# Second layer of an MLP in 64x64 quarters of the array, inside the attentions of the next batch

## The chip, the core and the metric

The kernel runs on one core of a Trainium2 chip. A core has TensorE (matmuls; in the profile PE, with its weight loads as PEld), VectorE (DVE), ScalarE (ACT), GpSimd (POOL) and SyncE (SP, which here only issues DMAs), each with an instruction queue of its own that is worked off in order; queues wait for one another through semaphores. Matmuls write to PSUM, which has eight banks of 512 float32 per partition, and an engine must read a result out of its bank before the bank takes another. The metric is the device time of one execution in microseconds (us).

## What is computed

Attention with normalised q and k over 8 batches and 12 heads (448 tokens, head size 64), and an MLP with tanh-GELU on its output:

```python
q_n, k_n = rmsnorm(q, g_q), rmsnorm(k, g_k)              # over the 64 of a head
attn = softmax(q_n @ k_n.T / sqrt(64))
x = (attn @ v)                                           # laid out as (3584 tokens, 768)
out = gelu_tanh(x @ w_in) @ w_out                        # 768 -> 2048 -> 768, float32 out
```

## The kernel before

Batches b = 0 to 7 run one after the other. A batch has an attention and a first layer; its second layer is worked off inside the attention of the next batch. `manual_schedule` is on: each engine's order is the order in which the code issues.

An attention (`attention`, L501; batch 0 has its own, `first_attention`) has 21 *units* (`unit`, L315): chunk c = 0 to 2 of four heads, key block t = 0 to 6. A unit is four matmuls of 64 rows x 64 columns of the array with 448 moving columns each, one per quarter of the array, into a two-bank tile `sc`; then one `exp` on ACT over both banks (896 elements per partition). When a chunk has its seven units, `products(b, c, 0)` sums the keys (matmuls with ones; where `key_sums` has added the keys on DVE before, only one group of four matmuls is left) and `products(b, c, 1)` multiplies with v: seven groups of four quarter matmuls. `turned`, `recips` and `quad_x` make x from them on DVE: two transposes, a reciprocal, a transpose, a multiplication into `xT`.

The first layer (`mm1_pair` L468, `mm1` L413) uses the full array, 128x128, six matmuls of 448 columns for each of 16 blocks f; a gelu on ACT writes g. The first two pairs of blocks use two-bank tiles, blocks 4 to 15 use one bank each from the pool `ps_m`.

The second layer (`mm2`, L434) has seven tiles of 128 tokens for two batches, three from an even batch and four from an odd one. For each tile and each half of the 768 output columns there are 16 full-array matmuls of 384 columns into one bank of `ps_m`, a copy to `osb` (L448 on DVE, L446 on ACT) and, after the second half, two DMAs on SP (L456). `m2_parts` makes a list of these matmuls, one *step* each; `attention` takes 96 (b = 1) or 112 (b = 2 to 7) of them from the list through `upto`, between the groups of units, in shares that are written out (`first`, `last`, `tail`, `shares`). Since an odd batch gives 128 steps and an even one 96, the attentions of batches 3, 5 and 7 begin in the middle of a list.

PSUM after the first batch: two single banks (`ps_m`) for the second layer and blocks 4 to 15 of the first, three two-bank tiles t0 to t2 (`rounds`) for units, products, the first two pairs of the first layer and a scratch tile in `rsqrt_last`. `pair` hands them out in turn:

```python
rounds.append(rounds.pop(0))
return rounds[-1]
```

The last batch's second layer (144 matmuls, L434) runs by itself at the end.

SP's queue holds, in the order of issue, the loads of q and k (L119), the transposes by DMA (L305) and the stores (L456).

Of the kernel before, what the change touches and what calls it, by code (L numbers as in the profile page):

```python
# [17 lines left out]
def kernel(  # L18
# [20 lines left out]
    R = 64  # L39
# [131 lines left out]
    roots, places = {}, {}  # L171
# [65 lines left out]
    def rsqrt_last(b):  # L237
# [3 lines left out]
        own = pair("root")[:, :, :4 * NT]  # L241
# [6 lines left out]
        for i in range(3):  # L248
            nc.vector.tensor_copy(z, y)
            nc.vector.tensor_mul(t, z, y)  # L250
            nc.vector.scalar_tensor_tensor(t, t, -0.5, ms, op0=ALU.mult, op1=ALU.mult)
            nc.vector.scalar_tensor_tensor(y, t, 1.5, y, op0=ALU.add, op1=ALU.mult)

# [61 lines left out]
    def unit(b, c, t):  # L315
# [12 lines left out]
        nc.scalar.activation(ex[:, t], sc[:, :, :S], AF.Exp, scale=scale, bias=shift)  # L328

# [29 lines left out]
    def products(b, c, what, lo=0, hi=NT):  # L359

        if lo == 0 and rounds:
# [19 lines left out]
    def turned():  # L381
        st = oas["st"] = stp.tile([128, 2, S // 32, 32], F32, tag="st", name="st")
        for r in range(2):
            nc.vector.transpose(st[:, r].rearrange("p a b -> p (a b)"), oas[0][r])  # L384

# [9 lines left out]
    def quad_x(b, c):  # L395
        if c == 0:
            xT[b] = xp.tile([128, HP, S], BF16, tag="xT", name="xT")
        if rounds:
            nc.vector.tensor_mul(
                xT[b][:, 2 * c:2 * c + 2], oas["o", 1][:, :, :S], oas["rb"]  # L400
            )
            return
# [5 lines left out]
    def mm1(b, f, cs=range(HP)):  # L408
        if cs[0] == 0:
            hs1["m"] = ps_m.tile([128, 512], F32, tag="mm", name="h")  # L410
        h = hs1["m"]
        for c in cs:
            nc.tensor.matmul(  # L413
                h[:, :S], win[:, c, f * 128:(f + 1) * 128], xT[b][:, c],
                start=(c == 0), stop=(c == HP - 1),
            )
        if cs[-1] < HP - 1:
            return
        nc.scalar.activation(  # L419
            g[:, f, (b % 2) * S:(b % 2 + 1) * S], h[:, :S], AF.Gelu_apprx_tanh  # L420
        )

    out_v = out.rearrange("(r t) d -> t r d", t=NT)
    osbs, by_act = {}, []

    def mm2(b, i, half, f, lo, hi):

        end = b + 1 == B and i + 1 == 2 * S // 128
# [4 lines left out]
        o, osb = osbs["ps"][:, :hi - lo], osbs[i]  # L433
# [6 lines left out]
        last = end and hi == d_model  # L440
        if last:

            nc.vector.tensor_copy(osb[:R, lo:hi], o[:R])
            nc.scalar.copy(osb[R:, lo:hi], o[R:])
        elif b + 1 == B and (lo == 0 or end) or by_act:
# [3 lines left out]
        if half == 0 and not end:  # L449
            return  # L450
        for j in range(2):
            col = i * 128 + j * R
            r = ((b // 2) * 2 + col // S) * R
            cols = slice(lo if end else 0, hi)
            eng = nc.scalar if last and j else nc.sync
            eng.dma_start(  # L456
                out_v[col % S // R, r:r + R, cols], osb[j * R:(j + 1) * R, cols]
            )

    def mm1_pair(i, cs=range(HP), b=0, js=range(2)):  # L460
# [11 lines left out]
        if cs[-1] == HP - 1 and js[-1] == 1:  # L472
            nc.scalar.activation(  # L473
                g[:, 2 * i:2 * i + 2, (b % 2) * S:(b % 2 + 1) * S], h[:, :, :S],
                AF.Gelu_apprx_tanh
            )

    early, late = range(HP - 2), range(HP - 2, HP)

    def m2_parts(b):  # L480
        tiles = range(3) if b % 2 == 0 else range(3, 7)
        order = [(i, half) for i in tiles for half in range(2)]
# [3 lines left out]
        parts = [(i, half, half * HD, (half + 1) * HD) for i, half in order]  # L486
        if b + 1 == B:
            i, half, lo, hi = parts.pop()
            parts += [(i, half, lo, lo + HD // 2), (i, half, lo + HD // 2, hi)]
        return [  # L490
            lambda part=part, f=f: mm2(b, part[0], part[1], f, *part[2:])
            for part in parts for f in range(nf)
        ]

    def attention(b, m2, quota, side, behind, ends):
# [3 lines left out]
        cuts = (0, 3, 6, 9, 11, 13, 16, 18, 21)  # L499
        groups = [units[i:j] for i, j in zip(cuts, cuts[1:])]  # L500
        first, last, tail = (23, 16, 4) if b > 1 else (18, 14, 3)  # L501
        sums_at, x_at = {3: 0, 6: 1}, {4: 0}
        shares = (0, 12, 24, 35, 45, 58, 69) if b > 1 else (0, 12, 25, 33, 41, 53, 61)
        spread = quota - first - last - tail
        given = 0

        def upto(k):
            nonlocal given
            while given < k:
                m2.pop(0)()  # L510
                given += 1

        before = []
        for i, group in enumerate(groups):
            for fn in side.get(i, ()):
                fn()
            if b == 1 and i == 3:
                by_act.append(b)
            for c, t in group:
                unit(b, c, t)  # L520
            for c, t in before:
                key_sums(b, c, t)
            if i in x_at:
                products(b, x_at[i], 1)
                quad_x(b, x_at[i])
            elif i in sums_at:
# [342 lines left out]
```

## Time and profile before

| | us |
|---|---|
| median of three runs | 411.4 (410.44, 411.4, 412.5) |
| profiled execution, span | 409.5 |
| PE busy | 400.1 |
| ACT busy | 277.3 |
| DVE busy | 258.1 |
| POOL busy | 121.8 |

The profile is one execution, taken apart from the three runs; its span goes from the first to the last instruction. The chain of waits is the work that ended last, followed back from the end; its pieces show what each stretch of the time was spent on. "L434 x12" means twelve instructions of line 434. The timeline merges neighbouring instructions of one kind: start, length, engine, line, operation, output and input, count. A group's line has its count, its busy time and the mean of one in ns.

### The profile page before, as it was taken

To read this page: it belongs to the slowest core of one execution; us is meant where nothing else is said; L and a number is where in the kernel's file an instruction comes from. 1 tells how busy PE (TensorE), PEld (TensorE's weight loads), DVE (VectorE), ACT (ScalarE), POOL (GpSimd) and SP (SyncE) were. 2 spreads that over 40 slices of the span, in tenths; PEclk is the share of its full clock that TensorE was granted. 3 is DMA by queue.
4 is the path that set the end of the run, shared out by engine and by line. 5 is a ranking of instruction groups with operands and counts; after the bars stand their busy time and mean duration, and the time that the engine had idled before them with its cause. 6 is when DMAs were issued, how large, how long until landed. Compare 5 with 4: busy or idle time off the path is not lost.

```text
span 409.5 us, 8104 instructions
## 1 busy us (share of the span) xinstructions
PE 400.1 (98%) x3337; PEld 209.5 (51%) x3337; DVE 258.1 (63%) x425; ACT 277.3 (68%) x374; POOL 121.8 (30%) x102
## 2 busy tenths in 40 slices
PE   8889999999999999999999999999999999999996
PEld 3354554554555555555555555555555555555564
DVE  5799729795699257964689366983598504990010
ACT  6896387867974789738876579748879249744301
POOL 5992307265004540082202740063400900000000
PEclk9899999999999999999999999999999999999999
DMA  8999996979612936239822948319822511111033
GB/s 280 256 232 219 202 189 226 218 182 284 107 41 65 268 56 186 58 76 267 168 68 51 213 104 196 77 30 250 137 47 74 111 31 38 40 40 40 0 78 78
DMA packets 65545, 54.07 MB, mean 132 GB/s; under 512 B 37348, under 2 KB 60516, under 8 KB 65508
## 3 DMA queue, kind: packets, MB, share of 16 engines
q1 hardware_dynamic: 53184, 41.48, 39.0%
q0 software_dynamic: 12096, 11.80, 18.3%
q8 instruction: 26, 0.43, 0.4%
q10 hardware_dynamic: 228, 0.28, 0.2%
q14 instruction: 11, 0.09, 0.1%
HBM read 45.61 MB, written 11.01 MB: 138 GB/s over the span
## 4 chain that ended last, share of the span: by engine, by line
PE 87%; DVE 4%; DMA 4%; ACT 2%; POOL 1%; issue 1%; DVEq 0%
PE o L434 36%; PE h L413 23%; PE t L375 9%; PE t L324 8%; PE t L468 8%; DMA kT<-nrmk 3%; ACT ex L328 1%; PE o L375 1%; DVE ss L164 1%; PE sc L324 1%; DMA rawq<-in_q_dram 1%; DVE st L384 1%; POOL nrmq L264 1%; DVE xT L404 1%; DVE rb L391 1%
## 5 line engine op out<-in xcount | busy, mean ns | idle before, releaser
L434 PE MATMUL o<-wout,g 128*128 128x384 bf16 (+1 forms) x912 | 156.8, 324 | 0.0
L328 ACT ACTIVATE ex<-t,shift 128x896 bf16<-128x896 f32 x147 | 137.7, 1005 | 24.1 <-PE t L324 22.7
L434 PEld LDWEIGHTS <-g 128*128 128x128 bf16 x912 | 83.6, 98 | 68.1 <-issue 19.2
L413 PE MATMUL h<-xT,win 128*128 128x448 bf16 x504 | 96.5, 353 | 0.0
L164 DVE TENSOR_REDUCE ss<-sq 128x14 f32<-128x896 f32 (+3 forms) x45 | 44.3, 998 | 48.4 <-ACT sq L157 45.5
L413 PEld LDWEIGHTS <-win 128*128 128x128 bf16 x504 | 49.3, 98 | 46.0
L419 ACT ACTIVATE g<-h 128x448 bf16<-128x448 f32 x84 | 45.6, 543 | 28.2 <-PE h L413 23.1
L448 DVE COPY osb<-o 128x384 f32<-128x384 f32 x47 | 25.6, 545 | 49.6 <-PE o L434 48.5
L652 POOL COPY mark<-es 1x1 bf16<-1x1 bf16 x6 | 1.1, 176 | 132.2 <-DVE es L346 132.2
L324 PE MATMUL t<-qT,kT 64*64 64x448 bf16 x588 | 39.9, 359 | 0.4 <-ACT g L473 0.2
L264 POOL TENSOR_TENSOR nrmq<-rawq,rinv 128x896 bf16<-128x896 f32 (+1 forms) x21 | 34.9, 1663 | 15.8 <-DVE o L232 10.2
L473 ACT ACTIVATE g<-t 128x896 bf16<-128x896 f32 x14 | 12.1, 914 | 39.9 <-PE t L468 39.9
L468 PEld LDWEIGHTS <-win 128*128 128x128 bf16 x264 | 25.7, 98 | 24.8 <-issue 2.0
L468 PE MATMUL t<-xT,win 128*128 128x448 bf16 x168 | 33.5, 352 | 0.0
L264 POOL TENSOR_TENSOR nrmk<-rawk,rinv 128x896 bf16<-128x896 f32 (+1 forms) x20 | 32.7, 1637 | 0.4 <-ACT rinv L196 0.4
L324 PEld LDWEIGHTS <-kT 64*64 64x64 bf16 x672 | 16.4, 106 | 29.9 <-issue 24.4
L375 PE MATMUL t<-ex,vb 64*64 64x448 bf16 x588 | 31.6, 350 | 0.0
L159 POOL TENSOR_TENSOR sq<-rawq 128x896 f32<-128x896 f32 (+1 forms) x9 | 13.6, 1517 | 51.1 <-DVE ss L164 25.2
L391 DVE STREAM_TRANSPOSE rb<-rc 128x896 f32<-128x896 f32 x24 | 26.7, 1111 | 0.8
L375 PEld LDWEIGHTS <-vb 64*64 64x64 bf16 x672 | 19.7, 107 | 12.7 <-issue 2.9
L384 DVE STREAM_TRANSPOSE st<-t 128x448 f32<-128x448 f32 x42 | 24.6, 625 | 1.3 <-PE t L375 1.3
L349 DVE TENSOR_TENSOR e<-ex 128x896 bf16<-128x896 bf16 x32 | 19.4, 606 | 8.7 <-ACT ex L328 8.5
(94 smaller groups left out, 343.4 us busy)
## 6 DMA issues: line engine op xcount, KB each, us to landing
out_dram<-osb SPq DMA_DIRECT2D x54, 192.0 KB, 2.7
rawq<-in_q_dram SPq DMA_DIRECT2D x23, 448.0 KB, 4.2
rawk<-in_k_dram SPq DMA_DIRECT2D x23, 448.0 KB, 5.5
vb<-in_v_dram POOLq DMA_DIRECT2D x8, 672.0 KB, 6.8
win<-in_moe_w_in_dram POOLq DMA_DIRECT2D x8, 384.0 KB, 14.3
wout<-in_moe_w_out_dram POOLq DMA_DIRECT2D x2, 1536.0 KB, 25.1
qT<-nrmq SPq DMA_TRANSPOSE x19, 5.0
kT<-nrmk SPq DMA_TRANSPOSE x19, 4.4
```

Source lines behind the costliest of these rows:

```text
L164: nc.vector.reduce_sum(sss[b][:, c, "qk".index(n), hs, ts], squares(b, c, n, hs, ts), axis=AX.X)
L264: eng.tensor_mul(nrms[n, b, c][:, ts].rearrange("p t a d -> p a t d"), raws[n, b, c][:, :, ts], root[:, :, ts].to_broadcast([P, 2, m, D]),)
L324: nc.tensor.matmul(sc[r * R:(r + 1) * R, a, :S], kT[rs, c, t, r], qT[b][rs, c, :, r], start=True, stop=True,)
L328: nc.scalar.activation(ex[:, t], sc[:, :, :S], AF.Exp, scale=scale, bias=shift)
L375: nc.tensor.matmul(o[r][a * D:(a + 1) * D], vb[b % 2][rs, 2 * c + a, i] if what else ones[rs], es[i][rs, a], start=(i == 0), stop=(i == n ...
L384: nc.vector.transpose(st[:, r].rearrange("p a b -> p (a b)"), oas[0][r])
L391: nc.vector.transpose(rb.rearrange("p r s -> p (r s)"), rc.to_broadcast([128, 2 * S // 32, 32]))
L413: nc.tensor.matmul(h[:, :S], win[:, c, f * 128:(f + 1) * 128], xT[b][:, c], start=(c == 0), stop=(c == HP - 1),)
L419: nc.scalar.activation(g[:, f, (b % 2) * S:(b % 2 + 1) * S], h[:, :S], AF.Gelu_apprx_tanh)
L434: nc.tensor.matmul(o, g[:, f, i * 128:(i + 1) * 128], wout[:, f, lo:hi], start=(f == 0), stop=(f == nf - 1),)
L448: nc.vector.tensor_copy(osb[:, lo:hi], o)
L468: nc.tensor.matmul(h[:, j, :S], win[:, c, f * 128:(f + 1) * 128], xT[b][:, c], start=(c == 0), stop=(c == HP - 1),)
```

## The change

Line numbers of the changed kernel differ: there a unit's matmul is L330, the products' L382, the second layer's L442 (L475 for the last batch), the first layer's L503.

- After the first batch all eight banks are four two-bank tiles t0 to t3 (`whole`). `pair` pops the tile at the head of the list `idle_pairs`; `give` puts a tile at its end when the code has issued the tile's last reader.
- `mm1` goes. All blocks of the first layer are done by `mm1_pair`, one gelu over two banks; only in the last pair the two blocks have a gelu each.
- The second layer of batches 0 to 6 is `mm2_quarters`. It takes two (tile, half) parts together into the two banks of one tile. A step is now four matmuls of 64x64 with 384 columns: rows of one half of the array go to bank 0, the other half's to bank 1. A first pass (p = 0) over the 16 blocks f has part n on row half n, a second pass (p = 1) on the other one, so both halves of the contraction are summed. Between the passes a nop on SP waits for the last matmul of the first pass, and the first weight load of the second pass waits for that nop. The copy is one instruction over 768 elements where both parts are of one tile of tokens (all but batch 0), and it is on DVE except for some of batch 1's attention.
- `mm2_last` does the last batch's second layer on the full array, the two halves of a tile of tokens in the two banks of one tile.
- `attention` follows a written list: U is a unit, a number so many steps, s and x the key sums and the products with v of a chunk. `add_keys` (the additions on DVE) stands ahead of the steps that follow it, `quad_x` behind the steps after the products. In batches 2 to 7 the products of chunk 1 move ahead of the last unit, and `recips` follows `turned` at once.

```diff
-    ps_m = ctx.enter_context(tc.tile_pool(name="ps_m", bufs=2, space=bass.MemoryType.PSUM))
     start = ctx.enter_context(ExitStack())
+    ps_m = start.enter_context(tc.tile_pool(name="ps_m", bufs=2, space=bass.MemoryType.PSUM))
...
-    rounds = []
+    whole, idle_pairs = [], []

     def pair(name):
-        if not rounds:
+
+        if not whole:
             return ps_s.tile([128, 2, 512], F32, tag="sc", name=name)
-        rounds.append(rounds.pop(0))
-        return rounds[-1]
+        return idle_pairs.pop(0)
+
+    def give(t):
+        if whole:
+            idle_pairs.append(t)
...
         nc.scalar.activation(ex[:, t], sc[:, :, :S], AF.Exp, scale=scale, bias=shift)
+        give(sc)
...
+    def mm2_quarters(b, parts, p, f):
+
+        if p == 0 and f == 0:
+            osbs["o"] = pair("o")
...
+        o = osbs["o"]
+        for n, (i, half) in enumerate(parts):
+            rs = slice((n ^ p) * R, (n ^ p) * R + R)
+            for c in range(2):
+                done = nc.tensor.matmul(
+                    o[c * R:(c + 1) * R, n, :HD],
+                    g[rs, f, i * 128 + c * R:i * 128 + (c + 1) * R],
+                    wout[rs, f, half * HD:(half + 1) * HD],
+                    start=(p == 0 and f == 0), stop=(p == 1 and f == nf - 1),
+                )
+                if p == 1 and f == 0 and n == 0 and c == 0:
+                    tc.add_manual_dep(done.ins, osbs["turn"].ins.name, SYNC)
+        if p == 0 and f + 1 == nf:
+            osbs["turn"] = nc.sync.nop(nofuse=True)
+            tc.add_manual_dep(osbs["turn"].ins, done.ins.name, SYNC)
+        if p == 0 or f + 1 < nf:
+            return
+        copy = nc.scalar.copy if by_act else nc.vector.tensor_copy
+        if parts[0][0] == parts[1][0]:
+            copy(osbs[parts[0][0]].rearrange("p (h d) -> p h d", h=2), o[:, :, :HD])
+        else:
+            for n, (i, half) in enumerate(parts):
+                copy(osbs[i][:, half * HD:(half + 1) * HD], o[:, n, :HD])
+        give(o)
+        for i, half in parts:
+            if half == 1:
+                store(b, i)
+
+    def mm2_last(i, lo, hi, f):
+
+        last, bank = hi == d_model and i == 6, lo == HD
         if f == 0:
-            osbs["ps"] = ps_m.tile([128, 512], F32, tag="mm", name="o")
+            if not bank:
+                osbs["o"] = pair("o")
...
+        o, osb = osbs["o"][:, int(bank), :hi - lo], osbs[i]
         nc.tensor.matmul(
             o, g[:, f, i * 128:(i + 1) * 128], wout[:, f, lo:hi],
             start=(f == 0), stop=(f == nf - 1),
         )
...
-        if cs[-1] == HP - 1 and js[-1] == 1:
+        if cs[-1] == HP - 1:
+            lo = 0 if len(js) == 2 else js[0]
             nc.scalar.activation(
-                g[:, 2 * i:2 * i + 2, (b % 2) * S:(b % 2 + 1) * S], h[:, :, :S],
-                AF.Gelu_apprx_tanh
+                g[:, 2 * i + lo:2 * i + js[-1] + 1, (b % 2) * S:(b % 2 + 1) * S],
+                h[:, lo:js[-1] + 1, :S], AF.Gelu_apprx_tanh
             )
+            if js[-1] == 1:
+                give(h)
...
+        if b > 1:
+            steps = ("U U U 16 U U 8 U 8 U U 8 U 8 U U 4 s0 4 U 8 U U 4 x0 4 U 8 "
+                     "U U 4 s1 4 U 8 U U 2 x1 U 10")
+        else:
+            steps = ("U U U 16 U U 8 U 8 U U 8 U 8 U U 4 s0 4 U 8 U U 4 x0 4 U 4 U 4 "
+                     "U U s1 4 U 3 U 3 U 2")
...
+            c = int(step[-1])
+            if step[0] == "s":
+                products(b, c, 0)
                 turned()
+                recips()
+            elif step[0] == "x":
+                products(b, c, 1)
+                held.append(c)
             else:
+                if u > 3:
+                    add_keys(u - 2 if u == 5 else u - 1)
+                upto(int(step))
+                while held:
+                    quad_x(b, held.pop())
...
-            elif f in (1, 3):
-                mm1_pair(f // 2, late, b)
-            elif f > 3:
-                mm1(b, f)
+            elif f + 1 == nf:
+                for j in range(2):
+                    mm1_pair(f // 2, range(HP), b, range(j, j + 1))
+            elif f % 2:
+                mm1_pair(f // 2, late if f < 4 else range(HP), b)
...
-            rounds += [
-                ps_t.tile([128, 2, 512], F32, tag=f"t{i}", name=f"t{i}") for i in range(3)
+            whole += [
+                ps_t.tile([128, 2, 512], F32, tag=f"t{i}", name=f"t{i}") for i in range(4)
             ]
-        attention(b + 1, m2, 96 if b == 0 else 112, plan(*side), plan(*behind), ends)
+            idle_pairs += whole
+        attention(b + 1, m2, plan(*side), plan(*behind), ends)
```

More of the change, by code (lines that the diff above doesn't have):

```diff
@@ L448, in mm2 @@
             nc.vector.tensor_copy(osb[:, lo:hi], o)
[L449 to L458, printed above, removed]
+        if bank:
+            give(osbs["o"])
+        if i == 6:
+            store(B - 1, i, slice(lo, hi), (nc.sync, nc.scalar if last else nc.sync))
+        elif hi == d_model:
+            store(B - 1, i)
     def mm1_pair(i, cs=range(HP), b=0, js=range(2)):
@@ L493, in m2_parts, with attention, upto, add_keys @@
         ]
[L495 removed]
+    def attention(b, m2, side, behind, ends):
         units = [(c, t) for c in range(NCH) for t in range(NT)]
[L499 to L509, printed above, removed]
[L510 to L527 removed]
+        firsts = (0, 3, 6, 9, 11, 13, 16, 18, 21)
+        if b > 1:
[4 more added lines that the diff above has]
+                     "U U s1 4 U 3 U 3 U 2")
+        tail, u, held = 4, 0, []
+        added_to = 0
+        def upto(n):
+            for _ in range(n):
+                m2.pop(0)()
+        def add_keys(n):
+            nonlocal added_to
+            while added_to < n:
+                key_sums(b, *units[added_to])
+                added_to += 1
+        for step in steps.split():
+            if step == "U":
+                if u in firsts:
+                    for fn in side.get(firsts.index(u), ()):
+                        fn()
+                    if b == 1 and firsts.index(u) == 3:
+                        by_act.append(b)
+                unit(b, *units[u])
+                u += 1
+                continue
+            c = int(step[-1])
+            if step[0] == "s":
+                products(b, c, 0)
```

96 lines of the change are left out of this document (43 added, 53 removed).

## The prediction

> **What bounds the kernel now.** I read the page first, then the chain of waits in order of time, then the timelines of DVE and ACT inside one attention. The page:
>
> ```profile
> span 409.5 us, 8104 instructions
> PE 400.1 (98%) x3337; PEld 209.5 (51%) x3337; DVE 258.1 (63%) x425; ACT 277.3 (68%) x374; POOL 121.8 (30%) x102
> PEclk9899999999999999999999999999999999999999
> PE 87%; DVE 4%; DMA 4%; ACT 2%; POOL 1%; issue 1%; DVEq 0%
> ```
>
> TensorE sets the end: 87% of the chain, at a full clock, so a wait of PE costs what it lasts. The busy 98% says little, as matmuls overlap; the chain gives each stretch its net length. Its columns are start, length, what:
>
> ```profile
> 196.01 0.69 PE t L324 x12
> ...
> 203.29 0.85 PE t L324 x12
> 204.15 2.06 PE o L434 x12
> ...
> 208.79 0.50 PE t L324 x8
> 209.29 1.32 PE t L375 x28
> ...
> 218.54 2.71 PE o L434 x16
> 221.25 2.97 PE t L375 x60
> ...
> 229.60 13.62 PE h L413 x72
> 243.22 0.69 PE t L324 x12
> ```
>
> One batch lasts 47.21 us (196.01 to 243.22). Twelve and sixteen L434 matmuls take 2.06 and 2.71: 0.1625 us each, plus 0.11 per block. Units: three groups of four quarters take 0.69, two take 0.50, so 0.19 a group plus 0.12. Seven groups of L375 right behind units take 1.32, 0.19 each and nothing more: there is no price between two quarter blocks, only between quarters and the full array.
>
> **The change, part by part.** Tiles t0 to t3 are the four two-bank tiles; `pair` takes the one given back longest ago.
>
> Removed: an attention has nine blocks of full-array L434, each entered for 0.11 and left for 0.12. After it, all of it is quarters until the first layer, one entry each way. 8 x 0.23 x 7 attentions = -12.9. The third unit's wait (0.85 against 0.69) loses its place: -1.0 over six attentions. The second layer itself: one group of four quarters of 384 columns does the work of one full matmul. The trace has no such group. Bounds: 0.1625 (the full matmul of the same 384 columns) and 0.19 (the quarter group of 448, eight instructions). At 448 the full array takes 13.62/72 = 0.189, equal to the quarter group, so both go by columns there; I take 0.1625, no change. The other end is 768 groups x 0.0265 = +20.
>
> The four weight loads of a group:
>
> ```profile
> L375 PEld LDWEIGHTS <-vb 64*64 64x64 bf16 x672 | 19.7, 107 | 12.7 <-issue 2.9
> ```
>
> One lasts 107 ns, and four fit under a 0.19 group, so they run beside each other and have 0.055 to spare in 0.1625. [...]
>
> What is added stands behind ACT and DVE. Rows of the timeline (start, length, engine, operation, the idle time before it in brackets), first around the end of a first layer and the kernel's last stage, then DVE's queue in one attention:
>
> ```profile
> 196.05 0.54 ACT L419 ACTIVATE g<-h 128x448 bf16<-128x448 f32 x1 [0.59 <-PE h L413]
> ...
> 197.90 2.80 ACT L328 ACTIVATE ex<-t,shift 128x896 bf16<-128x896 f32 x3
> ...
> 384.68 21.00 PE L434 MATMUL o<-wout,g 128*128 128x384 bf16 x144
> 384.88 0.54 ACT L419 ACTIVATE g<-h 128x448 bf16<-128x448 f32 x1 [0.59 <-PE h L413]
> 387.48 0.48 ACT L446 COPY osb<-o 128x384 f32<-128x384 f32 x1 [2.06 <-PE o L434]
> ```
>
> ```profile
> 209.96 0.58 DVE L349 TENSOR_TENSOR e<-ex 128x896 bf16<-128x896 bf16 x1
> 210.58 0.62 DVE L350 TENSOR_TENSOR es<-es,e 128x896 bf16<-128x896 bf16 x1
> 211.12 1.08 DVE L399 TENSOR_TENSOR xT<-t,rb 128x896 bf16<-128x896 f32 x1
> 212.12 0.55 DVE L448 COPY osb<-o 128x384 f32<-128x384 f32 x1
> ...
> 215.61 0.61 DVE L344 TENSOR_TENSOR es<-ex 128x896 bf16<-128x896 bf16 x1
> 216.14 1.17 DVE L384 STREAM_TRANSPOSE st<-t 128x448 f32<-128x448 f32 x2
> 217.35 0.33 DVE L390 RECIPROCAL rc<-st 128x28 f32<-128x28 f32 x1
> 217.71 1.11 DVE L391 STREAM_TRANSPOSE rb<-rc 128x896 f32<-128x896 f32 x1
> 218.75 0.58 DVE L349 TENSOR_TENSOR e<-ex 128x896 bf16<-128x896 bf16 x1
> 219.37 0.62 DVE L350 TENSOR_TENSOR es<-es,e 128x896 bf16<-128x896 bf16 x1
> 219.91 0.55 DVE L448 COPY osb<-o 128x384 f32<-128x384 f32 x1
> 220.38 2.07 DVE L346 TENSOR_TENSOR es<-es,ex 128x896 bf16<-128x896 bf16 x3
> ```
>
> An operation that needs the one before it starts 0.04 after its end (209.96 + 0.58, 210.58); that is my price of a signal between engines too, an estimate.
>
> Added, first: waits kept by the tile, not by its bank. In the built program a matmul into bank 1 waits for the reader of bank 0 where that reader was issued first. This meets (a) the last `mm1_pair` of b = 1 to 7, whose f = 15 waits for the gelu of f = 14, and (b) `mm2_last`, where the second half of tiles 3 to 6 waits for the ACT copy of the first.
>
> The last L413 matmul started 0.19 before 384.68; its gelu starts at 384.88, 0.39 later. With 0.54 and 0.04 for the signal back, f = 15 starts 0.97 after the last matmul of f = 14 instead of 0.19: 0.78 x 7 = +5.5. For (b): 16 matmuls from 384.68 put the sixteenth's start at 387.12; its copy starts 0.36 later; 0.36 + 0.48 + 0.04 - 0.16 = 0.72, x 4 = +2.9. Nothing covers either: PE has no other work in its order there.
>
> Added, second: the second layer's sums now live in the same four tiles as units and products, and DVE empties them late.
>
> The new copy of 768 elements is not in the trace: between one copy of 384 (0.55) and two (1.10), whose fixed part would count once in one copy; I take 0.95.
>
> Attention b (b = 1 is the second) works off what batches before it left. b = 2, 4, 6 begin with a fresh pair of parts, which ends at the 32nd, 64th and 96th step. Counted from the s0 matmuls, PE has 0.19, 4 steps, U, 8 steps (the pair ends), U U, 4 steps: 4 x 0.19 + 16 x 0.1625 = 3.36 until x0 asks for a tile, and the oldest given is that pair's. DVE: 0.39 to the transposes; then in the changed order two transposes, reciprocal, transpose, e, es, copy, as they stand from 216.14 to 219.91: 3.77; copy 0.95; signals 0.1: 5.2. Stall 1.85. x1, counted from the first of the two U before s1: exp 0.39 + 1.0 (three take 2.80 at 0.9 a start), add 0.53 (215.61 to 216.14), transposes to the end of rb 2.61 (216.14 to 218.75), copy 0.95, signals 0.15: 5.6 against 6 groups of 0.19 and 18 steps, 4.07. Stall 1.55. Then the sums of c = 2 wait for their last keys: from x1 on, DVE has e and es (1.16, 209.96 to 211.12), two adds (0.69 each), xT 1.00, an add 0.69: 4.2 against 7 groups, U and 10 steps, 3.15. Stall 1.05; before, 16 L434 and 28 products stood in between (218.54 and 221.25). Together 4.45 x 3 = +13.4.
>
> b = 3, 5, 7 begin in the middle of a pair, so it ends at the 16th, 48th and 80th step and copies fall better. There remain the sums of c = 2, where DVE reaches the transposes 0.9 after the s1 matmuls (0.39 + 1.0 + 0.04 + 0.53 from the first U, against U U and 4 steps, 1.03), and has 0.9 + 2.61 + 1.16 + 1.38 + 1.00 + 0.69 = 7.7 against PE's 6.2: 1.5. And the pair begun after 16 steps takes the third unit's tile: gelu, table load and three exps end 4.65 after 196.05, 5.04 after the last L413 matmul's start; PE is there after 0.31 + 0.57 + 2.6 + 0.38 = 3.9, plus about 0.4 that the units themselves waited: 0.7. Together 2.2 x 3 = +6.6.
>
> b = 1 has the same wait at c = 2 (1.5), and its first pair is emptied by two DVE copies behind key sums; by the x0 working 1.9; with small change 4.4 (bounds 0 and 6). Smaller waits of units on exps, which come at 0.9 apiece while three units and 16 steps take 3.17: 0.2 to 0.3, two or three in each of b = 2 to 7, +4.0 (0 to 6).
>
> The swap of row halves: SP's nop waits for the last first-half matmul and PE's next weights wait for SP. Two units (0.38) and the last group (0.16) cover 0.54; it needs about 0.36 and three signals of 0.04: 0.48. Zero; without that cover 0.5 x 24 = 12. Behind the nop on SP stand loads and transposes, which lose as little. ACT starts 35 gelus fewer, since two share one; it was not the bound.
>
> Sum: -12.9 - 1.0 + 5.5 + 2.9 + 13.4 + 6.6 + 4.4 + 4.0 = +22.9, against the profiled 409.5: 432.4. The median shown is 411.4, 1.9 above that span. Forecast 434.3, say 434.
>
> **The rivals.** *DVE keeps up*: tile waits vanish because the copy overlaps its neighbours better or PE asks later. Speaks for it: DVE is 63% busy; against it: its queue is dense exactly from sums to copy. Only the two bank waits remain: 411.4 - 13.9 + 8.4 = 406; it decides if the copy starts about 1.9 us sooner after s0 and 1.6 after s1. Chance 8%, 2 of these within 0.5% (about what a measurement can tell from no change). *Quarter groups of 384 hold at 0.19* because eight instructions or weight loads set the pace: 434 + 20 = 454. For: nothing shorter than 0.19 is in the trace; against: at 448 columns alone explain it. 9%. *SP is late*: the nop queues behind a store that waits for DVE's copy.
>
> ```profile
> SPq L456 <- DVE osb L448: 172.0, 20, 21.0
> ```
>
> SP stood 172 us at such stores, but the copy comes 3 us after a pair and the next nop 3.5 us after it; 1 us late in half of 24 swaps is 12: 446. 6%. *No switch saved*, if quarter blocks of different size still drain: 434 + 12.9 = 447; against it the 1.32 of L375. 2%.
>
> **How the numbers follow.** The forecast has 75%: 424 to 443, from tile waits of 60% to 140%. 8% lies on the other side. The range takes in SP's case and half the slow-group case: 421 to 448. Faster 0.06, same 0.02, slower 0.92.
>
> **What would show it.** Right: units, second layer and products (L330, L442, L382 there) in the chain without 0.11 steps between; gaps of 0.8 at f = 15; of 0.7 four times at the end; PE waiting on DVE before L382 for 1.8 and 1.5 in every second batch; batches of about 51 and 49 us. Wrong: L442 groups apart by 0.19; PE waiting on SP; or batches under 47.2, which would mean that the tiles come free in time.

## The result, and the profile after

The changed kernel takes 434.08 us in the median (432.76 to 437.53, four runs), the kernel before 410.92 on the same chip (409.66 to 412.5). The ratio is 1.058 (95% interval 1.053 to 1.063): slower, where the forecast was 434.0. The profiled execution of the changed kernel has a span of 432.7. In e5 and e10 below, one execution each (435.32 and 440.21) took over 1.5% longer than the fastest of its kernel; the ratios leave it out, and without it their medians are 429.52 and 433.2.

Page of the changed kernel: busy time, the chain that ended last by engine, and the group of the new copies:

```profile
PE 395.4 (91%) x5641; PEld 254.4 (59%) x5641; DVE 256.7 (59%) x404; ACT 273.5 (63%) x339; POOL 121.3 (28%) x102
...
PE 62%; DVE 17%; ACT 10%; issue 5%; DMA 4%; POOL 1%; DVEq 0%
...
L457 DVE COPY osb<-t 128x768 f32<-128x768 f32 x21 | 19.9, 945 | 21.4 <-PE t L442 21.2
```

VectorE now holds 17% of the chain, where it held 4%. The new copy of 768 elements takes 0.945 us. Below, the largest of PE's waits in the attentions and first layers (us in total, times, longest):

```profile
PE t L382 <- DVE osb L457: 9.0, 6, 1.7
PE t L382 <- DVE es L353: 7.7, 7, 1.3
PE t L503 <- ACT g L509: 4.4, 7, 0.6
```

These idle times count from the modelled end of the last matmul. What a wait costs is the distance of starts less what it would be without the wait, so the timeline is needed. Matmuls of the changed kernel (start, length, line, count, idle time before and its releaser), from attention 1 to the end:

```profile
55.69 0.76 PE L330 MATMUL t<-qT,kT 64*64 64x448 bf16 x12 [0.92 <-DVE rawk L141]
...
103.16 1.29 PE L503 MATMUL t<-xT,win 128*128 128x448 bf16 x6 [0.63 <-ACT g L509]
104.39 0.76 PE L330 MATMUL t<-qT,kT 64*64 64x448 bf16 x12
...
118.42 0.85 PE L442 MATMUL t<-wout,g 64*64 64x384 bf16 x16
120.93 1.52 PE L382 MATMUL t<-ex,vb 64*64 64x448 bf16 x28 [1.66 <-DVE osb L457]
...
128.12 0.52 PE L442 MATMUL t<-wout,g 64*64 64x384 bf16 x8
129.98 1.52 PE L382 MATMUL t<-ex,vb 64*64 64x448 bf16 x28 [1.33 <-DVE osb L457]
...
131.49 1.82 PE L442 MATMUL t<-wout,g 64*64 64x384 bf16 x40
134.16 0.38 PE L382 MATMUL t<-es,ones 64*64 64x448 bf16 x4 [0.84 <-DVE es L353]
...
155.51 1.08 PE L330 MATMUL t<-qT,kT 64*64 64x448 bf16 x12
...
170.25 0.85 PE L442 MATMUL t<-wout,g 64*64 64x384 bf16 x16
170.90 1.52 PE L382 MATMUL t<-ex,vb 64*64 64x448 bf16 x28
...
180.17 1.82 PE L442 MATMUL t<-wout,g 64*64 64x384 bf16 x40
183.27 0.38 PE L382 MATMUL t<-es,ones 64*64 64x448 bf16 x4 [1.28 <-DVE es L353]
...
204.61 0.76 PE L330 MATMUL t<-qT,kT 64*64 64x448 bf16 x12
...
355.97 0.38 PE L330 MATMUL t<-qT,kT 64*64 64x448 bf16 x4
...
404.99 2.76 PE L475 MATMUL t<-wout,g 128*128 128x384 bf16 x16
408.32 5.36 PE L475 MATMUL t<-wout,g 128*128 128x384 bf16 x32 [0.57 <-ACT osb L485]
...
426.10 2.80 PE L475 MATMUL t<-wout,g 128*128 128x192 bf16 x32 [0.57 <-ACT osb L485]
```

The same first units in the kernel before:

```profile
54.60 0.76 PE L324 MATMUL t<-qT,kT 64*64 64x448 bf16 x12 [0.22 <-ACT g L473]
...
101.53 0.76 PE L324 MATMUL t<-qT,kT 64*64 64x448 bf16 x12
...
337.57 0.38 PE L324 MATMUL t<-qT,kT 64*64 64x448 bf16 x4
```

Measured from first unit to first unit, an attention with its first layer took 47.21 before; it now takes 51.12 when b is even and 49.10 when b is odd (from b = 2 on). The 23.2 us between the two spans therefore lie here:

| stretch | before | after | more |
|---|---|---|---|
| to attention 1's first unit | 54.60 | 55.69 | 1.09 |
| attention 1 and its first layer | 46.93 | 48.70 | 1.77 |
| attentions 2 to 6 with theirs | 236.04 | 251.58 | 15.54 |
| attention 7 with its own, to the last stage | 47.11 | 49.02 | 1.91 |
| the last stage's matmuls | 21.00 | 23.91 | 2.91 |

### The profile page after: what moved, and what is told of

It reads as the page before. It is cut to its first block, busy times and chain, and to the rows that moved or that the text cites. A ratio compares the mean times of both kernels' runs of the same rounds, so it can differ in the third digit from the quotient of the medians.

```text
span 432.7 us, 12710 instructions
## 1 busy us (share of the span) xinstructions
PE 395.4 (91%) x5641; PEld 254.4 (59%) x5641; DVE 256.7 (59%) x404; ACT 273.5 (63%) x339; POOL 121.3 (28%) x102
## 4 chain that ended last, share of the span: by engine, by line
PE 62%; DVE 17%; ACT 10%; issue 5%; DMA 4%; POOL 1%; DVEq 0%
PE t L503 28%; PE t L442 17%; ACT ex L334 6%; PE t L382 6%; PE t L475 5%; PE t L330 4%; DMA kT<-nrmk 3%; DVE st L391 3%; DVE es L353 3%; DVE ss L168 2%; DVE rb L400 2%; ACT L868 2%; ACT g L509 2%; DVE osb L457 1%; PE o L382 1%
## 5 line engine op out<-in xcount | busy, mean ns | idle before, releaser
L442 PE MATMUL t<-wout,g 64*64 64x384 bf16 x3072 | 147.6, 323 | 1.7 <-ACT ex L334 1.5
L503 PE MATMUL t<-xT,win 128*128 128x448 bf16 x672 | 129.6, 352 | 4.8 <-ACT g L509 4.4
L442 PEld LDWEIGHTS <-g 64*64 64x64 bf16 x3072 | 106.8, 107 | 25.7 <-issue 3.9
L503 PEld LDWEIGHTS <-win 128*128 128x128 bf16 x768 | 74.3, 98 | 77.7 <-issue 9.3
L509 ACT ACTIVATE g<-t 128x896 bf16<-128x896 f32 (+1 forms) x63 | 51.8, 833 | 80.2 <-PE t L503 80.2
L330 PE MATMUL t<-qT,kT 64*64 64x448 bf16 x588 | 47.5, 351 | 2.6 <-DVE rawk L141 1.3
L382 PE MATMUL t<-ex,vb 64*64 64x448 bf16 x588 | 32.0, 350 | 9.0 <-DVE osb L457 9.0
L330 PEld LDWEIGHTS <-kT 64*64 64x64 bf16 x672 | 23.5, 107 | 18.7 <-issue 12.0
L382 PEld LDWEIGHTS <-vb 64*64 64x64 bf16 x672 | 23.3, 106 | 18.2 <-issue 11.7
L457 DVE COPY osb<-t 128x768 f32<-128x768 f32 x21 | 19.9, 945 | 21.4 <-PE t L442 21.2
L408 DVE TENSOR_TENSOR xT<-t,rb 128x896 bf16<-128x896 f32 x21 | 22.8, 1084 | 1.7 <-PE t L382 1.3
L475 PE MATMUL t<-wout,g 128*128 128x384 bf16 (+1 forms) x144 | 21.6, 308 | 2.3 <-ACT osb L485 2.3
```

The source lines that it names most:

```text
L330: nc.tensor.matmul(sc[r * R:(r + 1) * R, a, :S], kT[rs, c, t, r], qT[b][rs, c, :, r], start=True, stop=True,)
L382: nc.tensor.matmul(o[r][a * D:(a + 1) * D], vb[b % 2][rs, 2 * c + a, i] if what else ones[rs], es[i][rs, a], start=(i == 0), stop=(i == n ...
L442: done = nc.tensor.matmul(o[c * R:(c + 1) * R, n, :HD], g[rs, f, i * 128 + c * R:i * 128 + (c + 1) * R], wout[rs, f, half * HD:(half + 1) ...
L457: copy(osbs[parts[0][0]].rearrange("p (h d) -> p h d", h=2), o[:, :, :HD])
L475: nc.tensor.matmul(o, g[:, f, i * 128:(i + 1) * 128], wout[:, f, lo:hi], start=(f == 0), stop=(f == nf - 1),)
L503: nc.tensor.matmul(h[:, j, :S], win[:, c, f * 128:(f + 1) * 128], xT[b][:, c], start=(c == 0), stop=(c == HP - 1),)
```

## The experiments

Each is the changed kernel with the edit shown. Times are medians. The kernel before had 410.1, 410.4 and 410.3 in the three groups of runs (e1 to e4, e5 to e8, e9 to e12) and 410.9 beside the changed kernel, so a difference of medians between groups is uncertain by some 0.8; ratios are to the kernel before. The last column is from the profiles: the time from attention 2's first unit to the last stage's first matmul. It leaves out the start and attention 1, which differ by several us between executions of the same program (last section).

| run | us (range) | ratio (95%) | attentions 2 to 7 |
|---|---|---|---|
| kernel before | 410.92 (409.66 to 412.5) | 1 | 283.15 |
| changed kernel | 434.08 (432.76 to 437.53) | 1.058 (1.053 to 1.063) | 300.60 |
| e1 | 432.01 (429.85 to 434.5) | 1.052 (1.049 to 1.056) | 300.65 |
| e2 | 431.66 (430.26 to 433.58) | 1.052 (1.049 to 1.055) | 298.09 |
| e3 | 445.73 (444.66 to 446.17) | 1.086 (1.083 to 1.088) | 310.56 |
| e4 | 428.45 (427.33 to 429.3) | 1.044 (1.041 to 1.047) | 294.93 |
| e5 | 429.9 (428.62 to 435.32) | 1.047 (1.045 to 1.050) | 296.71 |
| e6 | 436.84 (435.31 to 437.94) | 1.064 (1.061 to 1.066) | 300.57 |
| e7 | 411.87 (411.06 to 413.82) | 1.004 (1.002 to 1.006) | 281.37 |
| e8 | 424.33 (423.78 to 426.03) | 1.035 (1.032 to 1.037) | 293.61 |
| e9 | 433.68 (433.26 to 435.16) | 1.057 (1.055 to 1.059) | 300.61 |
| e10 | 433.29 (432.96 to 440.21) | 1.057 (1.054 to 1.060) | 300.57 |
| e11 | 411.67 (410.55 to 413.4) | 1.004 (1.002 to 1.006) | 282.11 |
| e12 | 431.84 (431.13 to 432.97) | 1.052 (1.050 to 1.055) | 297.70 |

### e1: the last stage's halves in tiles of their own

```diff
-            if not bank:
-                osbs["o"] = pair("o")
+            osbs["o"] = pair("o")
...
-        o, osb = osbs["o"][:, int(bank), :hi - lo], osbs[i]
+        o, osb = osbs["o"][:, 0, :hi - lo], osbs[i]
...
-        if bank:
-            give(osbs["o"])
+        give(osbs["o"])
```

> Theory (a tile keeps its waits whole): in the last stage each half of the second layer sits in a tile of its own, so the second half no longer waits for ScalarE's copy of the first. The changed kernel shows that wait four times, 2.3 us of idle time by the profile, and by the prediction 0.72 each from start to start: 4 x 0.72 = 2.9 less, 431.2 (430.5 to 432), and no row in which the last stage waits for ScalarE's copy. Rival (the chip waits for nothing there, the records only show it so, or the next tile in line is no sooner free): 434, and the idle time stays under another name.

432.01: 2.1 less by the medians, at the edge of the expected 430.5 to 432. The profiled execution keeps its span of 432.7, because attention 1 takes 52.86 in it and 48.70 in the changed kernel's (last section); the stage itself shows the effect. Timeline of e1's last stage:

```profile
407.86 21.00 PE L474 MATMUL t<-wout,g 128*128 128x384 bf16 x144
```

All 144 matmuls run in one piece of 21.00, as before the change, where the changed kernel needed 23.91: 2.9 less, as the theory says. The tile kept the wait, not the bank.

### e2: one gelu for the last pair

```diff
-            elif f + 1 == nf:
-                for j in range(2):
-                    mm1_pair(f // 2, range(HP), b, range(j, j + 1))
             elif f % 2:
```

> Theory (a tile keeps its waits whole): the first layer's last pair gets one gelu of 896 in place of two of 448, as all its other pairs have, so the matmuls of f = 15 wait for nobody: 0.78 back in each of seven batches. But the one gelu ends later than the second of the two did (0.916 against 0.543, 0.37), and the first exponentials of the next attention stand behind it; so between 7 x 0.41 = 2.9 and 7 x 0.78 = 5.5 less: 428.6 to 431.2, taken as 430.5, with the row of the wait of 4.4 us for the gelu gone. Rival (the quarter groups are slower, and this wait lies over other idle time): 434 within 1.

431.66: 2.4 less, which misses the expected 428.6 to 431.2; the row of the wait for the gelu is gone. ACT at the end of that first layer, first in e2, then in the changed kernel:

```profile
105.05 0.92 ACT L509 ACTIVATE g<-t 128x896 bf16<-128x896 f32 x1 [1.35 <-PE t L503]
...
105.99 1.28 ACT L865 ACT_TABLE_LOAD   x1
```

```profile
104.50 0.54 ACT L509 ACTIVATE g<-t 128x448 bf16<-128x448 f32 x1 [1.39 <-PE t L503]
...
105.06 1.28 ACT L868 ACT_TABLE_LOAD   x1
```

The table load that the exponentials wait for starts 0.94 after the gelu's start instead of 0.56. So of the 0.78 per batch ScalarE takes 0.38 back, and 0.40 is left; the batches shrink from 51.12 to 50.70 and from 49.10 to 48.69. By these rows the lower end of the expectation, 0.41 a batch, is the right one. That the median shows less than seven times this fits a chance wait in attention 1, which e2's profile has too (under e6).

### e3: full-array matmuls in the same tiles

```diff
-        for n, (i, half) in enumerate(parts):
-            rs = slice((n ^ p) * R, (n ^ p) * R + R)
...
-        if p == 0 and f + 1 == nf:
-            osbs["turn"] = nc.sync.nop(nofuse=True)
-            tc.add_manual_dep(osbs["turn"].ins, done.ins.name, SYNC)
+        i, half = parts[p]
+        nc.tensor.matmul(
+            o[:, p, :HD], g[:, f, i * 128:(i + 1) * 128],
+            wout[:, f, half * HD:(half + 1) * HD], start=(f == 0), stop=(f == nf - 1),
+        )
```

> The two-bank tiles, their order, copies and waits stay as in the changed kernel; only the second layer's matmuls are 128 x 128 again, each half of the output in its own bank, with no swap and no SyncE step. Theory (a change between quarters and the full array costs 0.11 in and 0.12 out, the groups themselves cost the same): the nine blocks of an attention pay again, 8 x 0.23 x 7 = 12.9, of which the waits for tiles that stand behind a block swallow a part (seven to eight waits for VectorE's copy and for key sums, 0.1 to 0.2 each, some 3): 442 to 447, taken as 444; the mean spacing within a block stays 0.1625. Rival A (quarters of 384 columns are the slow part, the change of mode costs nothing): 434 less what the quarters lose, below 430. Rival B (the SyncE step costs): 0.4 at most in each of 22 swaps, 2.9 in all by the idle time of weight loads behind it, so 434 - 2.9 + 10 = 441.

445.73, 11.7 more than the changed kernel. Matmuls of e3:

```profile
110.24 1.47 PE L440 MATMUL t<-wout,g 128*128 128x384 bf16 x8
111.65 0.38 PE L330 MATMUL t<-qT,kT 64*64 64x448 bf16 x4
111.96 1.47 PE L440 MATMUL t<-wout,g 128*128 128x384 bf16 x8
...
123.47 1.52 PE L382 MATMUL t<-ex,vb 64*64 64x448 bf16 x28 [1.10 <-DVE osb L448]
```

Eight matmuls take 1.41 from start to start, 8 x 0.1625 and 0.11; the group of four quarters behind them takes 0.31, 0.19 and 0.12. Both steps are back at the price that the prediction put on them. Attentions 2 to 7 together take 10.0 more. Part of it disappears in the waits: the one at x0 is 1.10 here and 1.66 in the changed kernel. Rivals A and B fall.

### e4: the pairs' copies on ScalarE

```diff
-        copy = nc.scalar.copy if by_act else nc.vector.tensor_copy
+        copy = nc.scalar.copy if by_act or b > 0 else nc.vector.tensor_copy
```

> The copies of the second layer's pairs go to ScalarE in all batches but the first. Theory (the tiles come back late because VectorE has sums, transposes and key additions ahead of the copy): the row in which the products wait for VectorE's copy, 9.0 us of idle time, goes for the most part; ScalarE is 63% busy and takes 18 copies of some 0.8 us more, in front of exponentials, which gives a part back: 5 less, 429 (427 to 431). Rival A (not VectorE's queue but the length of the pair keeps the tile: the copy is merely the last link): within 1 of 434. Rival B (ScalarE becomes the bound between units): 18 x 0.8 = 14 more in exponentials that the units wait for, 440 or more.

428.45, 5.6 less. It is 21 copies, not 18, of 0.805 each. Two of PE's waits in attention 3 of e4:

```profile
160.73 1.49 PE L442 MATMUL t<-wout,g 64*64 64x384 bf16 x32 [0.75 <-SPq L451]
180.93 0.38 PE L382 MATMUL t<-es,ones 64*64 64x448 bf16 x4 [1.82 <-DVE es L353]
```

The 9.0 of waiting for the copy have gone but for 0.6, now under ScalarE's name; attention 2 falls from 51.12 to 48.48 (103.32 to 151.80). But attention 3 grows from 49.10 to 50.48: the sums of chunk 2 wait 1.82 instead of 1.28, and for the first time PE itself waits for the swap. So here the cure in one attention (2.64 less) is partly paid in the next (1.38 more).

### e12: the copies ahead of the key additions, on VectorE

```diff
             else:
+                upto(int(step))
                 if u > 3:
                     add_keys(u - 2 if u == 5 else u - 1)
-                upto(int(step))
```

> The pairs' copies stay on VectorE, but in attentions 1 to 7 each step's matmuls and the copy they end in are issued ahead of that step's key additions instead of behind them (on VectorE up to two of 0.6 each). Theory (the place in VectorE's queue and not the engine keeps the tile): the wait at x0 shrinks by one or two additions, some 0.6 to 1.2 in three batches, that at x1 less; the sums of chunk 2 lose nothing or some tenths: 2 to 4 less, 431 (430 to 432.5), which is less than ScalarE's 5.6. Rival (order does not matter, VectorE's whole load does): 434 within 0.7, since the additions it puts off are then late for the sums.

431.84, 2.2 less. A wait of attention 1 and the one at x0 of attention 2 in e12:

```profile
67.11 0.84 PE L442 MATMUL t<-wout,g 64*64 64x384 bf16 x16 [2.52 <-SPq L451]
...
120.54 1.52 PE L382 MATMUL t<-ex,vb 64*64 64x448 bf16 x28 [0.46 <-DVE osb L457]
```

At x0 the idle time falls by 1.20, the two additions that stood ahead of the copy (e and es); at x1 (1.34) and at the sums (0.85) nothing changes. So at x0 it is the copy's place in VectorE's queue that costs. An even attention becomes 1.2 shorter and an odd one 0.24 longer. The row at 67.11 is a wait for the swap: SP's nop stood behind loads of q and k (65.10 to 67.00) which waited for VectorE.

### e5: the products of chunk 1 back in the tail

```diff
-                     "U U 4 s1 4 U 8 U U 2 x1 U 10")
+                     "U U 4 s1 4 U 8 U U U 12")
```

> One part undone: in attentions 2 to 7 after the first of them the products of chunk 1, second half (x1), go from the ordered steps back to the tail, where they stood before between the last units and the sums of chunk 2; the ten steps they leave join the last piece. Theory (the sums of chunk 2 wait for VectorE's last key additions because the 28 products no longer stand in front of them, and x1 itself waits for a copy): of the row in which products wait for key sums, 7.7 us, the six later ones go or shrink by some 0.7 to 1.0 each, and the waits for the copy at x1 with them: 4 to 7 less, 429 (427 to 431). Rival (the waits only move behind x1 in the tail, as VectorE has the same work to do): 433 to 435, with the wait under x1's or the quad's name.

429.9, 4.2 less (3.9 in attentions 2 to 7): within the expectation, but partly for the rival's reason. In the profiled execution attention 1 is lengthened by the wait that the last section takes apart, so only later rows are read, in attentions 2 and 3:

```profile
134.56 2.14 PE L442 MATMUL t<-wout,g 64*64 64x384 bf16 x48 [1.48 <-DVE osb L457]
...
186.82 0.38 PE L382 MATMUL t<-es,ones 64*64 64x448 bf16 x4 [0.48 <-DVE es L353]
```

The sums of chunk 2 wait 0.48 in attention 3 instead of 1.28, and in attention 2 next to nothing. The wait for the copy at x1 did not go: it moved to the next pair of the second layer, which now asks for that tile (1.48 for 1.33).

### e6 and e10: no swap

```diff
-            rs = slice((n ^ p) * R, (n ^ p) * R + R)
+            rs = slice(n * R, n * R + R)
...
-                if p == 1 and f == 0 and n == 0 and c == 0:
-                    tc.add_manual_dep(done.ins, osbs["turn"].ins.name, SYNC)
-        if p == 0 and f + 1 == nf:
-            osbs["turn"] = nc.sync.nop(nofuse=True)
-            tc.add_manual_dep(osbs["turn"].ins, done.ins.name, SYNC)
```

> The row halves do not swap and the SyncE step is gone: each half of the output sums the same 64 rows of every block of 128 in both passes and leaves the other 64 out; the number of matmuls, their shapes, tiles and copies are those of the changed kernel. Theory (the step costs next to nothing, since the matmuls of a pass are queued ahead): the weight loads show 2.9 us of idle time behind it in 17 swaps, of which the matmul queue hides most: 0.5 less, 433.6 (433 to 434). Rival (the loss of the change is in the swap: SyncE answers late, behind its stores): at least the 2.9 less, 431 or below.

436.84, 2.8 more: both expected less. Its attention 2 has the changed kernel's rows and length, so the loss is at the start, where there is a row that the changed kernel's profile lacks:

```profile
64.85 1.94 PE L442 MATMUL t<-wout,g 64*64 64x384 bf16 x30 [3.33 <-DMA wout<-in_moe_w_out_dram]
```

The missing swap is not its cause: e2, which has the swap, shows it too, 3.00 at 64.49, with the weights issued at 31.80 and landed 32.6 later. In the changed kernel (issue of the weights' second half, time to landing of the two halves, and the second pair's first group) these weights come just in time: 32.35 + 29.9 = 62.25.

```profile
32.35 1.21 POOL L684 DMA_DIRECT2D wout<-in_moe_w_out_dram  x1
```

```profile
DMA to landing us min/median/max: 21.1/25.5/29.9
```

```profile
62.43 1.47 PE L442 MATMUL t<-wout,g 64*64 64x384 bf16 x32
```

e9 and e10 are the changed kernel and e6 with that load issued directly behind the first:

```diff
-            lambda: w_out_part(0), lambda: load_v(1, 0, HP),
+            lambda: w_out_part(0), lambda: w_out_part(1), lambda: load_v(1, 0, HP),
...
-            lambda: w_out_part(1), lambda: released()),
+            lambda: released()),
```

> One load moved: the second half of the second layer's weights is issued right behind the first (in the changed kernel 5.3 us later, at 32.35, landing 29.9 later at 62.25, while its first matmul starts at 62.43), ahead of the values of attention 1, which are wanted at 70.8. Theory (in the changed kernel's order these weights are wanted at the 33rd step and not at the 49th as before, and in some executions they land some 3 us late): the profile without that wait stays at its 432.7, the runs lie closer together, at 432 to 435, their median 433.5, none above 436 for this. Rival (their landing never decides, the spread is the start's): spread and median stay, 434 within 1.

> The kernel without the swap (each half of the output sums the same 64 rows of every block of 128 in both passes and leaves the other 64 out) with the weights' second half issued sooner. Its profile without this showed 3.33 us of waiting for those weights and the same 51.12 us for a batch as the changed kernel. Theory (the swap and its SyncE step cost next to nothing, and the 436.8 was the weights' landing): 433.0, within 0.7 of the changed kernel with the same load moved. Rival (the lack of a swap costs by itself, or hinders the groups): 435.5 to 437 again.

e9 has 433.68, e10 433.29: without the late weights, leaving the swap out gains 0.4, less than the runs differ among themselves, and attentions 2 to 7 take 300.57 without it (e6 and e10) and 300.60 with it. The swap is as good as free in this kernel. For the changed kernel itself the moved load changes the median by 0.4 only, and four runs each can't say whether the spread has shrunk.

### e7, e8 and e11: all waits mended

e7 takes e1, gives f = 14 and f = 15 a tile and a gelu each, puts the copies on ScalarE except for those that end tile 6, and uses these lists (attention 1, even, odd):

```diff
+            "U U U 16 U U 16 U U U 16 U U U 4 s0 12 U U U 4 x0 4 U 4 U 4 U U s1 4 U 3 U 3 U 2"
+            "U U U 16 U U 8 U U 8 U 8 U 8 U U 4 s0 4 U 8 U U 4 x0 4 U 8 U U 4 s1 4 U 8 U U U 12"
+            "U U U 16 U 8 U U 8 U 6 U U 9 U 5 s0 4 U 8 U x0 U 8 U U 8 U 4 s1 4 U U 8 U U U 12"
```

> The quarters stay; all the waits that the prediction added are attacked at once: own tiles for each half of the last stage, own tiles and gelus for f = 14 and f = 15, the pairs' copies on ScalarE (on VectorE for tile 6's pairs alone), x1 back in the tail, and the units and steps put in another order. Theory (switches saved 13.9, waits cost 36.8): the waits fall by about 26, to less than the saving: 408.5 (406.5 to 411), at or just below the kernel before, with the rows of waits for VectorE's copy, for the gelu and for ScalarE's copy gone from the matmuls' waits. Rival A (with these waits gone ScalarE, 63% busy and with 17 more copies of 0.8, sets the pace of the units): 414 or more, with exponentials as the units' releaser. Rival B (quarter groups lose by themselves): 415 to 420, with no wait to show for it.

411.87: 22 less than the changed kernel, above the expected 406.5 to 411, and still 0.4% (0.2 to 0.6%) above the kernel before. PE's largest wait in it, and first units:

```profile
PE t L382 <- DVE es L353: 2.0, 4, 1.5
```

```profile
104.59 0.76 PE L330 MATMUL t<-qT,kT 64*64 64x448 bf16 x12
...
339.50 1.08 PE L330 MATMUL t<-qT,kT 64*64 64x448 bf16 x12
```

From attention 2 to 7 it needs 234.91 where the kernel before needs 236.04, and in attention 7 and its first layer 46.46 for 47.11. What it lacks is lost ahead of 104.59, 3.06 later than before. So this kernel wins 1.8 in the steady part and loses 3.1 ahead of it. Of the 3.1, 1.2 lie ahead of attention 1's first unit, where e1 and the changed kernel, the same program up to there, differ as much (54.35 and 55.69), so that part need not be the change's; 1.8 lie in attention 1. A version with the old second layer in attention 1 was not tried.

> The mended kernel with the same load moved. Its profile showed no wait for these weights, so theory: no change, 411.9 within 1. Rival (in the executions that are not profiled it waits there too): 409 to 410.5, under the kernel before.

e11 has 411.67: these weights no longer matter there.

e8 is e7 with e3's edit:

> The mended kernel, its second layer again 128 x 128 with each half of the output in its own bank. Theory (a change of mode costs 0.11 and 0.12, and with few waits left nothing swallows it): nine blocks in seven attentions and as many edges as the new order of steps has, about 8 x 0.23 x 7 = 12.9 and up to 1 more: 13 to 14 above the mended kernel, 422 if that has 408.5; more than the 11 to 12 by which the same edit slowed the changed kernel. Rival (the 11 to 12 were a price of the full matmuls themselves, or of waits that the edit moved): the same 11 to 12 or less.

424.33. That is 12.5 above e7 by the medians and 13.4 by the profiled spans (424.2 and 410.8), against 11.7 for the same edit in the changed kernel: more, as the theory says, though by the medians only just, and 0.5 short of its range. In attentions 2 to 7 the edit costs 12.2 here and 10.0 there.

## Why the prediction was right

The waits came where the prediction put them, and of the sizes it gave them, but for attention 1. By stretch its steps add up as follows; an attention has eight switches less (1.84), and from attention 2 on 0.17 for the third unit less and 0.67 of small waits more. That the forecast of 434.0 and the median of 434.08 agree to a tenth is luck: errors of 0.5 and 0.8 have opposite signs, and attention 1 differs by more than that from one execution to the next.

| stretch | predicted | measured |
|---|---|---|
| start and attention 1 | -1.84 + 0.78 + 4.4 = 3.3 | 1.09 + 1.77 = 2.9 |
| an even attention (three) | -1.84 - 0.17 + 0.78 + 4.45 + 0.67 = 3.9 | 51.12 - 47.21 = 3.9 |
| an odd attention (three) | -1.84 - 0.17 + 0.78 + 2.2 + 0.67 = 1.6 | 49.10 - 47.21 = 1.9 |
| last stage | 2.9 | 2.9 |

- *Switches, -12.9*: right. e3 shows the two steps at 0.11 and 0.12, and e8, where little is left to hide them, costs 12.5 to 13.4. The rival that no switch is saved is out. The steps in e3's trace put 0.23 on a change there and back.
- *The second layer itself, 0*: right. Sixteen quarter matmuls, four groups, take 0.65 from 170.25 to the products at 170.90: 0.1625 a group, as on the full array (32 matmuls in 5.36 from 408.32: 31 steps of 0.1625 and the last one's own 0.33). The rival of 454 is out. One weight load of 64 columns lasts 107 ns in the changed kernel's trace too (L442), and a group has four, so they run beside each other.
- *f = 15 behind the gelu, 5.5*: the wait is there, 0.63 idle in each of seven batches, and the tile makes it: in e7, where each of the two blocks has a tile and a gelu of its own, the row is gone. But e2 shows that taking it away by one gelu for both returns only about 0.4 each, because ScalarE pays the rest.
- *The last stage*: the tile makes it, and e1 removes it.
- *Even attentions, 4.45*: at x0, 120.93 less 118.42 and four groups of 0.1625 is 1.86 (predicted 1.85); at x1, 129.98 less 128.12 and two groups is 1.53 (1.55); at the sums, 134.16 less 131.49 and ten groups is 1.04 (1.05). e12 shows that at x0 VectorE's queue ahead of the copy does it, e4 that without that queue both waits for the copy go but for 0.6 in all.
- *Odd attentions, 2.2*: the sums of chunk 2 wait 183.27 less 180.17 and ten groups, 1.47 (1.5). That the stretch is 0.25 longer than predicted is not explained by this; no run took its smaller waits apart.
- *Attention 1, 4.4*: the one term that is visibly mis-sized. With 1.84 saved and 0.78 for the gelu, its growth of 1.77 leaves 2.8 of waits of its own; at its first unit PE idles 0.92 where it idled 0.22. Together 3.5. What is off is the wait for the first pair's tile, put at 1.9: by the order in which tiles are given back, the unit behind the second pair's first eight groups takes that tile, and it starts at 64.31, only 0.58 later than 62.43 and eight groups of 0.1625. The sums of chunk 2 wait 82.06 less 79.09 and seven groups of 0.19, 1.64 (1.5). In e1, the same program up to the last stage, the first pair's tile costs 3.17 (last section). So 1.9 lies between what two executions show, and the 2.9 in the table would have been 5.7 by e1's profile. The odd attentions' 0.8 in all made up for the shortfall.
- *The swap, 0*: right for the changed kernel by e6 and e10. SP does come late where copies are moved: PE's matmuls lose 1.0 us by it in e4 and 2.5 at one place in e12, not the 12 of the rival.

## What to carry to other kernels

A tile that two results share stayed busy here until the last reader of both was done, so before pools are merged, list for each tile who empties it and what stands ahead of that reader in its queue: here 13 us of saved mode switches were paid for with an estimated 36 us of waits, 13 and the 23 by which the kernel became slower. Count a repeated stage from its first instruction to the next one's first: idle times alone understated the loss here (1.66 for 1.86 at x0), and medians also move with chance waits elsewhere in the program. A wait that is taken away must be followed to where the tile is asked for next (e4, e5).

## What the runs showed that was not expected

Attention 1 of the quarters' order has waits of about 3 us that come and go between executions. One is for the weights' second half, wanted from the second pair on (62.43): it landed at 62.25 in the changed kernel's profile, but in time for 64.85 only in e6 and for 64.49 only in e2. The other is the wait for the first pair's tile. In e1 an addition on VectorE, ahead of the two copies that empty this tile (L460), lasted three times as long where GpSimd squared at the same time. First e1, then the changed kernel:

```profile
62.46 1.94 POOL L163 TENSOR_TENSOR sq<-rawq 128x896 f32<-128x896 f32 x1 [16.59 <-DMA rawq<-in_q_dram]
...
62.97 1.92 DVE L353 TENSOR_TENSOR es<-es,ex 128x896 bf16<-128x896 bf16 x1
...
64.81 1.01 DVE L460 COPY osb<-t 128x384 f32<-128x384 f32 x2
...
65.87 0.59 PE L330 MATMUL t<-qT,kT 64*64 64x448 bf16 x4 [3.00 <-DVE rawk L141]
...
66.20 2.74 PE L442 MATMUL t<-wout,g 64*64 64x384 bf16 x32
```

```profile
62.70 0.63 DVE L353 TENSOR_TENSOR es<-es,ex 128x896 bf16<-128x896 bf16 x1
...
63.53 1.68 POOL L163 TENSOR_TENSOR sq<-rawq 128x896 f32<-128x896 f32 x1 [16.32 <-DMA rawq<-in_q_dram]
...
64.31 0.38 PE L330 MATMUL t<-qT,kT 64*64 64x448 bf16 x4 [0.41 <-DVE rawk L141]
...
64.49 1.50 PE L442 MATMUL t<-wout,g 64*64 64x384 bf16 x32
```

In both, the unit (L330) starts about 0.05 after the copies end, at 65.82 and 64.25; the row names a one-element write (L141) that VectorE issued at the same time. Counted from the second pair's first eight groups, which begin at 61.40 and 62.43, it is late by 3.17 in e1 and by 0.58 in the changed kernel. Of the difference, 1.3 is the longer addition, 1.0 that PE came to this place earlier, and 0.3 that VectorE came to it later.

The addition lasts 1.91 to 1.92 in e1, e5, e10 and e12, where a square had begun before it and was still running, and 0.62 to 0.63 in the nine other profiles of the changed kernel and the experiments. In e3 and e11 the square begins second, during the addition, and it is the square that grows, from 1.68 to 1.97 and 2.08. In e1 the addition, the second to begin, ended 0.49 after the square, which itself lasted 1.94 where the changed kernel's lasted 1.68. No run was made to force either order, so what makes them longer is not shown.

Such a wait can cost more than it lasts, which the prediction did not reckon with. Behind it in e1, the 32 quarter matmuls take 2.74 where the changed kernel's take 1.50, and the granted clock of TensorE is 0.51 from 65.80 to 68.80, against 1.00 from 64 to 66 in the changed kernel. So attention 2 begins at 107.21 instead of 104.39: 1.56 later for the unit and some 1.2 for these matmuls. The clock is lower behind the waits of 2.99 in e5 (0.69 from 67.30 to 70.20) and 3.33 in e6 (0.68 from 64.80 to 67.50) too, but not behind those of 3.00 in e2 and 2.52 in e12 (1.00); what decides it no run shows.
